# Attention's values, loaded once and placed a second time by a copy

## The chip, the cores and the metric

The kernel runs on one core of one Trainium2 chip. The metric is device time in microseconds (us); three runs of the kernel before gave a median of 1081.24 us, with 1080.13 and 1085.15 as the lowest and the highest. A core has five engines with a queue each: PE (TensorE, the matmuls; its weight loads are listed as PEld), DVE (VectorE), ACT (ScalarE), POOL (GpSimd) and SP (SyncE, which here only issues transfers). Each works through its own instructions in the order in which the program wrote them, and semaphores make one engine wait for another. Transfers run on 16 DMA engines, whichever queue issues them.

## What is computed

Sparse attention, and then a mixture of experts over its output. Attention has 8 batches, 8 heads, 576 positions and a head size of 64. A query of the first four heads sees the 32 positions up to and including its own; one of the last four sees every fourth position, again 32 of them.

```python
mask_plain = (rel >= 0) & (rel < window)                                  # window = 32
mask_dil = (rel >= 0) & (rel < window * dilation) & (rel % dilation == 0) # dilation = 4
scores = np.where(masks[None], scale * q @ k.T, -1e9)
attn = exp(scores - max);  attn = attn / (sum(attn) + 1e-09)
x = (attn @ v)                       # rows of 8 heads * 64 = 512, 4608 of them
# each row then goes to two of 8 experts: relu(x @ w1[e]) @ w2[e], weighted and added
```

After a regrouping of the positions, a dilated head is four plain ones, each on every fourth position. In both cases a query needs at most the keys and values of its own block of 32 and of the block before.

## The kernel before

**Groups and stages.** The batches are taken two at a time (four pairs). A pair has two groups: the dilated heads (even groups, `ty` = 1) and then the plain heads (odd groups, `ty` = 0), so there are 8 groups, and each has three stages, 24 in all (stage `k`, group `g` = `k` // 3). A stage multiplies queries and keys (`qk`, L371, on top of masks that L360 puts into PSUM), takes the maximum and the difference on DVE (L376, L377) and the exponential on ACT (`expo`, L382); in the next round PE transposes the exponentials and ACT brings them back (`ptr`, L396 and L397), PE multiplies them with the values (`pv`, L414), and DVE divides by the sum (L421 to L426). A round later the result is moved, stored and transposed, and the gate's matmul is done (`move_x` L434, `store_x` L439 and L441, `x_transpose` L449, `gate_mm` L471).

**The values.** A matmul in `pv` works on 64 queries' worth of two blocks at once. It contracts over 128 partitions: 64 keys for the first 32 queries (`w` = 0) and 64 keys for the second 32 (`w` = 1). The values stand in a tile of two halves along the partition, one for each `w`, and where a partition belongs to the other `w` there is zero, so that one matmul gives both results side by side. Before the change, even partitions belong to `w` = 0 and odd ones to `w` = 1. With blocks of 32 numbered along the sequence, `w` = 0 needs blocks 2n - 1 and 2n, and `w` = 1 needs 2n and 2n + 1: every block is used twice. The host lays the values out as such windows, with every block in it twice (`windows`), and a load fills every second partition. There is one tile for dilated groups (`VD`, shown as `vd`, 4680 fp32 on a partition for each `w`) and two for plain groups (`VP`, shown as `vp`, 2340 each). Zeros are written once: into `vd` by ACT (L139), into `vp` by DVE and POOL (L197).

**What sets the order.** The program is unrolled, and the order in which it calls the engines is the order of their queues. Work that isn't part of a stage hangs on numbered slots, two for each round (`at(slot, f)`, carried out by `fillers`). Group `g` begins at slot `s0` = 6 `g`; the loads of the next group's values hang on `s0` + 3, + 5 and + 7, those of the keys and queries two groups ahead on `s0` + 7 and later. All these loads are issued by SP, in one queue with the stores of the results, which wait for the stages. At slots 2, 4 and 5 stand `setup_a`, `setup_b` and `setup_c`, which prepare constants and the token table on POOL and DVE: `setup_b` begins with POOL's L232 to L242 (`tokc`, `tc`), and DVE's L237 and the lines after it read them. Three pieces of the table's padding follow at slots 6, 12 and 18 (`pads`, L281 to L284).

From about slot 17 on, the rows that are finished get their experts (`gate`), and POOL scatters an entry of a table for each (`fill_slots`, L628), at most four scatters a round; before the first of them POOL copies one element of the latest result (`pace`, L306), and so waits for it. Later POOL gathers the rows of the experts (L770, L778). The experts' matmuls (`up` L826, `down_tile` L868) begin when attention is over, at 227.2 us, and take the rest of the time.

Of the kernel before, what the change touches and what calls it, by code (L numbers as in the profile page):

```python
# [9 lines left out]
F32 = mybir.dt.float32  # L10
# [15 lines left out]
U = 4  # L26
# [14 lines left out]
US_W2 = 3.0, 3.5  # L41
LAG = 15
US_X = (17, 52)


@with_exitstack
def attention_moe_kernel(ctx, tc, qt, kp, kd, vpl, vdl, w_gate, w_noise, noise, w1, w2, out, CAPS=(1216, 1216, 1216, 1184, 1184, 1152, 1152, 1152), SPLITS=(0, 384, 896)):
    nc = tc.nc
    tensor, vector, scalar, gpsimd, sync = nc.tensor, nc.vector, nc.scalar, nc.gpsimd, nc.sync
# [32 lines left out]
    sm = actx.enter_context(tc.tile_pool(name="sm", bufs=2))  # L82
# [13 lines left out]
    VP = [vp.tile([128, 2, 9, 4, 65], F32, name=f"vp{i}") for i in range(2)]  # L96
    VD = dp.tile([128, 2, 9, 4, 2, 65], F32, name="vd")
# [5 lines left out]
    def qk_loads(g, parts=1):  # L103
        u, ty = g // 2, 1 - g % 2
        for i in range(parts):
            n = KN[ty] // parts
            for y in range(2):
                yield lambda i=i, n=n, y=y: sync.dma_start(
                    KT[ty][y:128:2, y, n * i:n * i + n], (kp, kd)[ty][u, y:128:2, n * i:n * i + n])
            n = 4 * S // parts  # L110
            yield lambda i=i, n=n: sync.dma_start(QT[ty][:, n * i:n * i + n], qt[u, ty, :, n * i:n * i + n])

    def v_loads(g):
        u, ty = g // 2, 1 - g % 2
        if ty:
            d = VD.rearrange("p w j h y c -> p w (j h y c)")
            n = d.shape[2] // 3
            for i in range(3):
                for w in range(2):
                    yield lambda i=i, w=w: sync.dma_start(d[w:128:2, w, n * i:n * i + n],  # L120
                                                          vdl[u, w:128:2, n * i:n * i + n])
        else:
            for b in range(2):
                for w in range(2):
                    yield lambda b=b, w=w: sync.dma_start(VP[b][w:128:2, w].rearrange("p j h c -> p (j h c)"),
                                                          vpl[u, b, w:128:2])

    scalar.preload_act_table_set("natural_log_exp_and_others")  # L130
    none = acon.tile([128, 1], F32, name="none")
# [2 lines left out]
    gpsimd.memset(KT[1][:, 1], 0.0)  # L134
    for f in qk_loads(0, 2):
        f()

    def clear_by_copy(t):
        scalar.copy(t, none.to_broadcast(list(t.shape)) if len(t.shape) == 2 else  # L139
                    none.unsqueeze(2).unsqueeze(3).to_broadcast(list(t.shape)))  # L140

    VF = VD.rearrange("p w j h y c -> p w (j h y c)")
    for w in range(2):
        clear_by_copy(VF[:, w])
    clear_by_copy(KT[0][:, 0])


# [45 lines left out]
            p0 = 64 * x + 32 * h  # L193
            gpsimd.tensor_copy(m[p0:p0 + 32, 6 * h], m0[p0:p0 + 32, 1])
    vector.memset(KT[0][:, 1], 0.0)
    for b, w, eng in ((0, 0, vector), (0, 1, gpsimd), (1, 0, gpsimd), (1, 1, gpsimd)):
        eng.memset(VP[b][:, w], 0.0)  # L197
    tri = consts.tile([128, 128], BF, name="tri")
    ones = consts.tile([128, 128], BF, name="ones")
    wg = acon.tile([128, 4, 32], F32, name="wg")  # L200
# [151 lines left out]
    SB, PE_, PT, XG, XT, GS = {}, {}, {}, {}, {}, {}  # L352
# [25 lines left out]
        SB[k] = a  # L378

    def expo(k):  # L380
        p = sm.tile([128, 6, 64, 2], F32, name="pe")
        scalar.activation(p.rearrange("p j c w -> p j w c"), SB.pop(k).rearrange("p y (j w) c -> p (y j) w c", w=2),  # L382
                          AF.Exp, scale=0.125)
        PE_[k] = p

# [510 lines left out]
    def plan(t, f, lag=None):  # L896

        if lag is not None:
            plan(t, lambda: plan(now[0] + lag, f()))
        else:  # L900
            heappush(due, (t, next(turn), f))
# [9 lines left out]
    def at(kb, *fs):  # L911
        fill.setdefault(kb, []).extend(fs)
# [3 lines left out]
    for g in range(2 * U):  # L916
        s0 = 6 * g
        if g + 1 < 2 * U:
            for i, f in enumerate(v_loads(g + 1)):
                at(s0 + 3 + 2 * (i // 2), f)  # L920
        if g + 2 < 2 * U:
            for i, f in enumerate(qk_loads(g + 2, 2)):
                at(s0 + 7 + 2 * (i // 3), f)
    fronts = {6 * u + 6 + st: (u, st) for u in range(U) for st in range(3)}
    def idx_late(before, a, b, then):
        while any(g in gens for g in before):
            yield 1
        for _ in range(IX_WAIT):
            yield 1
        idx_dma(0, a, b)  # L930
        then()
# [20 lines left out]
    def split_first(bi, t):  # L952
        xsplit(0, bi, t)()
        done[bi] += 1

    def x_block(bi):
        gens.insert(0, first_blocks(bi))
        if bi == 0:
            later(max(L0 + SL_W1 + 3 - slot[0], 0), lambda: new_x(0, 0))
            return  # L960
        for i, t in enumerate(range(BLS[0][bi][0], BLS[0][bi][1])):
            plan(US_X[bi - 1] + 3.0 * i, lambda t=t: split_first(bi, t))

# [3 lines left out]
    at(29, lambda: (new_idx(0), gens.append(idx_late(list(gens), 0, SPLITS[1], lambda: x_block(0)))))  # L967
    at(41, lambda: gens.append(idx_late(list(gens), SPLITS[1], SPLITS[2], lambda: x_block(1))))
    at(2, setup_a)
    at(4, setup_b)  # L970
    at(5, setup_c)
    for f in v_loads(0):
        f()
    for f in qk_loads(1):
        f()

# [18 lines left out]
    for kc in range(4):  # L995
        a, b = ((-3, 2), (-2, 3), (4, 6), (5, 7))[kc]
# [11 lines left out]
    for i in range(NS + 2):  # L1008
# [18 lines left out]
        if i < NS:  # L1027

            expo(i)
# [48 lines left out]
    for e in range(E):  # L1078
# [7 lines left out]
        t, at_ = start, {}  # L1086
# [4 lines left out]
        t = start if first else at_[0, 1]  # L1091
# [37 lines left out]
        if not last:  # L1129
            t = start + (42 if first else 20)  # L1130
            plan(t, lambda e=e: (new_idx(e + 1), idx_dma(e + 1, 0, CAPS[e + 1])))
            t = max(t + (14 if first else 9), at_[0, 1])
# [3 lines left out]
            t = at_[0, 2] + dur(e, 2, False)  # L1136
# [20 lines left out]
    with tc.If(big > 0):  # L1157
        with tc.For_i(0, E, 1) as r:
            e = nc.values_load(ci[0:1, bass.ds(r, 1)], min_val=0, max_val=E - 1)
            n = nc.values_load(ci[0:1, bass.ds(r + E, 1)], min_val=0, max_val=T - min(CAPS))  # L1160
# [22 lines left out]
def _layouts(q, k, v):  # L1183
    import numpy as np

    def heads(a, ty):

        a = a.reshape(U, 2, H, S, D)
        if ty == 0:
            return a[:, :, 0:4].reshape(U, 2, 2, 2, S, D).transpose(0, 5, 2, 1, 3, 4).reshape(U, 128, 2, 2, S)  # L1190
        a = a[:, :, 4:8].reshape(U, 2, 4, S // 4, 2, 2, D)
        return a.transpose(0, 6, 5, 1, 2, 4, 3).reshape(U, 128, 2, 4, S // 2)

    def windows(a):

        n = a.shape[1] // 64
        a = np.pad(a, ((0, 0), (32, 0)) + ((0, 0),) * (a.ndim - 2))
        p = np.arange(128)[:, None]
        at = 64 * np.arange(n) + p // 2 + 32 * (p % 2)
        return a[:, at]  # L1200

    qt = np.stack([heads(q, ty).reshape(U, 128, 4 * S) for ty in range(2)], 1)
    pad = ((0, 0),) * 4 + ((32, 0),)
    kp = np.pad(heads(k, 0), pad).reshape(U, 128, -1)
    kd = np.pad(heads(k, 1), pad).reshape(U, 128, -1)
    def with_ones(a):
        return np.concatenate([a, np.ones(a.shape[:-1] + (1,), np.float32)], -1)

    vpl = windows(with_ones(v[:, 0:4].transpose(0, 2, 1, 3))).reshape(U, 2, 128, -1)

    dil = v[:, 4:8].reshape(U, 2, 4, S // 4, 2, 2, D).transpose(0, 1, 4, 3, 2, 5, 6).reshape(U, S, 4, 2, D)
    vdl = windows(with_ones(dil)).reshape(U, 128, -1)
    return {"qt": qt, "kp": kp, "kd": kd, "vpl": vpl, "vdl": vdl}


# [18 lines left out]
```

## Time and profile before

| | us |
|---|---|
| median of three runs | 1081.24 |
| lowest and highest | 1080.13 and 1085.15 |
| span of the profiled execution | 1086.8 |
| attention: first mask matmul (L360) to the experts' first matmul | 9.6 to 227.2 |
| experts | 227.2 to the end |

The profiled execution is one run, recorded instruction by instruction. Its own time beside the span is not listed apart; its span is 5.6 us over the median of the runs. Of the span PE is busy for 1011.7 us (93%), DVE for 465.7, ACT for 319.4 and POOL for 534.5. The granted clock is the share of TensorE's full clock that it was given; its mean is 0.963.

A row of the timeline has the start, the time taken, the engine, the line, the operation, what it writes and reads, and the count; in brackets stands how long the engine was idle before it, and what ended that. A row of waits has the engine and line that waited, what for, the total, the count and the longest. "issue" means a wait for nothing that the profile shows, and "remote" a semaphore whose sender it doesn't show.

### The profile page before, as it was taken

To read this page: it belongs to the slowest core of one execution; us is meant where nothing else is said; L and a number is where in the kernel's file an instruction comes from. 1 tells how busy PE (TensorE), PEld (TensorE's weight loads), DVE (VectorE), ACT (ScalarE), POOL (GpSimd) and SP (SyncE) were. 2 spreads that over 40 slices of the span, in tenths; PEclk is the share of its full clock that TensorE was granted. 3 is DMA by queue.
4 is the path that set the end of the run, shared out by engine and by line. 5 is a ranking of instruction groups with operands and counts; after the bars stand their busy time and mean duration, and the time that the engine had idled before them with its cause. 6 is when DMAs were issued, how large, how long until landed. Compare 5 with 4: busy or idle time off the path is not lost. (4 is left out here: it accounts for less than half of the span.)

```text
span 1086.8 us, 18768 instructions
## 1 busy us (share of the span) xinstructions
PE 1011.7 (93%) x7274; PEld 855.7 (79%) x7275; DVE 465.7 (43%) x1060; ACT 319.4 (29%) x609; POOL 534.5 (49%) x727
## 2 busy tenths in 40 slices
PE   6896877778989999999999999999999999999996
PEld 4774655567878989988997889788978888888885
DVE  7673635635225444344434352435353434343221
ACT  6673534622113322222223131312131222222110
POOL 7004243455776655755644564466455645553112
PEclk9998887878999999999999999999999999999999
DMA  8898687455255243533533352426242623453123
GB/s 280 313 315 278 194 283 257 151 164 186 43 96 129 54 109 85 109 84 86 91 85 85 86 131 50 102 64 135 38 112 52 137 39 108 75 119 72 24 28 45
DMA packets 79214, 132.95 MB, mean 122 GB/s; under 512 B 31648, under 2 KB 41296, under 8 KB 77840
## 3 DMA queue, kind: packets, MB, share of 16 engines
q1 hardware_dynamic: 56768, 92.56, 27.6%
q0 software_dynamic: 22352, 39.15, 19.6%
q8 instruction: 58, 0.95, 0.4%
q14 instruction: 36, 0.29, 0.1%
HBM read 92.11 MB, written 39.54 MB: 121 GB/s over the span
## 5 line engine op out<-in xcount | busy, mean ns | idle before, releaser
L826 PE MATMUL up<-x,w1h 128*128 128x512 f32 (+4 forms) x1536 | 396.7, 344 | 10.9 <-issue 8.2
L778 POOL DMA_INDIRECT g<-xs,ixi x258 | 269.7, 1045 | 84.0 <-issue 78.6
L826 PEld LDWEIGHTS up<-x,w1h 128*128 128x128 f32 x1536 | 273.1, 189 | 37.2 <-issue 8.7
L826 PE MATMUL up<-x,w1l 128*128 128x384 f32 (+4 forms) x768 | 263.4, 343 | 0.0
L868 PE MATMUL dn<-w2h,hh 128*128 128x512 f32 x576 | 225.5, 392 | 0.0
L868 PE MATMUL dn<-w2l,hh 128*128 128x512 f32 x576 | 224.7, 390 | 0.0
L868 PE MATMUL dn<-w2h,hl 128*128 128x512 f32 x576 | 224.6, 390 | 0.0
L832 DVE SCALAR_TENSOR_TENSOR hl<-up,hh 128x384 fp32r<-128x384 f32 (+2 forms) x192 | 106.7, 557 | 249.1 <-ACT hh L830 187.0
L830 ACT ACTIVATE hh<-up 128x384 fp32r<-128x384 f32 (+4 forms) x192 | 94.6, 498 | 298.7 <-PE up L826 248.7
L845 POOL DMA_INDIRECT out_rows<-y,ixs x67 | 107.3, 1602 | 141.4 <-DVE y L877 119.0
L826 PEld LDWEIGHTS up<-x,w1l 128*128 128x128 f32 x768 | 145.4, 189 | 11.8
L877 DVE TENSOR_SCALAR y<-dn,ixs 128x512 f32<-128x512 f32 x63 | 47.3, 751 | 188.2 <-PE dn L868 163.5
L868 PEld LDWEIGHTS dn<-w2h,hl 128*128 128x128 f32 x576 | 108.4, 188 | 22.7
L868 PEld LDWEIGHTS dn<-w2h,hh 128*128 128x128 f32 x576 | 108.5, 188 | 22.0
L868 PEld LDWEIGHTS dn<-w2l,hh 128*128 128x128 f32 x576 | 108.5, 188 | 21.8
L797 ACT CAST x<-xr 128x512 fp32r<-128x512 f32 x67 | 40.5, 605 | 216.0 <-DVE xr L795 175.8
L306 POOL COPY spacer<-hh 1x1 f32<-1x1 f32 x72 | 26.4, 366 | 131.9 <-ACT hh L830 131.6
L628 POOL DMA_INDIRECT tab<-en,si x72 | 71.8, 998 | 36.1 <-issue 16.2
L798 DVE TENSOR_TENSOR x<-xr,x 128x512 fp32r<-128x512 f32 x67 | 44.7, 667 | 17.9 <-ACT x L797 12.4
L371 PE MATMUL s<-kt,qt 128*32 128x128 f32 x1152 | 41.2, 288 | 9.9 <-DMA qt<-in_qt 5.4
L371 PEld LDWEIGHTS s<-kt,qt 128*32 128x32 f32 x1152 | 32.5, 115 | 20.3 <-issue 19.6
L708 DVE TENSOR_TENSOR w1l<-ws,w1h 128x1024 fp32r<-128x1024 f32 x32 | 38.8, 1218 | 20.8 <-ACT w1h L706 10.9
(186 smaller groups left out, 867.2 us busy)
## 6 DMA issues: line engine op xcount, KB each, us to landing
ws<-in_moe_w SPq DMA_DIRECT2D x36, 512.0 KB
ws<-in_moe_w SPq DMA_DIRECT2D x112, 128.0 KB
out_rows<-zero SPq DMA_DIRECT2D x38, 256.0 KB
vd<-in_vdl SPq DMA_DIRECT2D x24, 390.0 KB
vp<-in_vpl SPq DMA_DIRECT2D x16, 585.0 KB
qt<-in_qt SPq DMA_DIRECT2D x14, 576.0 KB
xs<-x SPq DMA_DIRECT2D x24, 256.0 KB
kt<-in_kd SPq DMA_DIRECT2D x16, 320.0 KB
```

The lines of the kernel that those rows point to most:

```text
L371: tensor.matmul(s[32 * qd:32 * qd + 32, e], lhsT=QV[ty][:, b, x, 32 * ub:32 * ub + 32], rhs=KV[ty][:, :, b, x, 32 * ub:32 * ub + 64], star ...
L628: ins = gpsimd.indirect_dma_start(out=tab, out_offset=bass.IndirectOffsetOnAxis(ap=si[:, kq, t:t + 1], axis=0), in_=en[:, kq, t], in_offse ...
L708: return lambda: vector.tensor_tensor(b, s, a.bitcast(F32), op=OP.subtract)
L778: gpsimd.indirect_dma_start(out=g[:, j], out_offset=None, in_=xq, in_offset=bass.IndirectOffsetOnAxis(ap=IX[e][1][:, r0 // 32 + j:r0 // 32 ...
L797: scalar.copy(xh[:, :, o:o + rn], xr[:, :, 0:rn])
L798: return lambda: vector.tensor_tensor(xl[:, :, o:o + rn], xr[:, :, 0:rn], xh[:, :, o:o + rn].bitcast(F32), op=OP.subtract)
L826: tensor.matmul(p[:, 0:n], lhsT=a[:, 128 * f:128 * f + 128], rhs=b[:, kc, 0:n], start=(i == 0), stop=(i == 11))
L830: scalar.activation(hh[:, f, 0:n], p[:, 0:n], AF.Relu)
L832: vector.scalar_tensor_tensor(hl[:, f, 0:m], p[:, 0:m], 0.0, hh[:, f, 0:m].bitcast(F32), op0=OP.max, op1=OP.subtract)
L845: ins = gpsimd.indirect_dma_start(out=out, out_offset=bass.IndirectOffsetOnAxis(ap=sc[0:rn, t, 1:2], axis=0), in_=y[0:rn], in_offset=None, ...
L868: tensor.matmul(p[0:rn], lhsT=a[:, f, o:o + rn], rhs=b[:, f % 2], start=(i == 0), stop=(i == 23))
L877: vector.tensor_scalar(y[0:rn], p[0:rn], wsc, None, op0=OP.mult)
```

## The change

**Layout.** The contraction's partitions are ordered anew: partitions 0 to 63 belong to `w` = 0 and 64 to 127 to `w` = 1, and each quadrant of 32 partitions holds one block: 2n - 1 and 2n for `w` = 0, then 2n and 2n + 1 for `w` = 1. `expo` writes the exponentials in that order. The host lays out every block once (`blocks`), 64 rows instead of 128.

**Loads.** `v_load` fills the second quadrant (partitions 32 to 63, `w` = 0) and the fourth (96 to 127, `w` = 1), with a transfer of 32 partitions for each. A dilated group has three parts, a plain group two, and the parts stand at the same slots as before.

**The second place.** `v_repeat` fills the third quadrant with a GpSimd copy of the second (`w` = 1). The first quadrant takes the fourth's blocks, one step along: in groups 0 to 3 (`VCOPY` = 4) by another GpSimd copy, in groups 4 to 7 by a load from DRAM, issued with the other loads. The copies hang on the slot three after the load's. Those of group 0 stand ahead of the first round, behind the masks in POOL's queue.

**Zeros.** ACT clears, of `vd`, the halves that belong to the other `w` and the first block's place. For `vp`, `clear_plain` does the same on DVE and POOL; that of the second plain tile moves to slot 3. The loads of group 0 no longer stand behind ACT's clearing of the whole `vd`.

```diff
+    def v_load(g, i):
+        b, j0, j1 = v_parts(g)[i]
+        n = VB[1 - g % 2]
+        for w in range(2):
+            sync.dma_start(VF[1 - g % 2][b][32 + 64 * w:64 + 64 * w, w, n * j0:n * j1],
+                           v_source(g, b)[32 * w:32 * w + 32, n * j0:n * j1])
+
+    def v_repeat(g, i, w):
+        b, j0, j1 = v_parts(g)[i]
+        n, t = VB[1 - g % 2], VF[1 - g % 2][b]
+        if w:
+            gpsimd.tensor_copy(t[64:96, 1, n * j0:n * j1], t[32:64, 0, n * j0:n * j1])
+            return
+        j0 = max(j0, 1)
+        dst, src = t[0:32, 0, n * j0:n * j1], (n * (j0 - 1), n * (j1 - 1))
+        if g < VCOPY:
+            gpsimd.tensor_copy(dst, t[96:128, 1, src[0]:src[1]])
         else:
+            sync.dma_start(dst, v_source(g, b)[32:64, src[0]:src[1]])
...
     for f in qk_loads(0, 2):
         f()
+    for i in range(3):
+        v_load(0, i)
...
-    VF = VD.rearrange("p w j h y c -> p w (j h y c)")
-    for w in range(2):
-        clear_by_copy(VF[:, w])
+    clear_by_copy(VF[1][0][0:64, 1])
+    clear_by_copy(VF[1][0][64:128, 0])
+    clear_by_copy(VF[1][0][0:32, 0, 0:VB[1]])
...
-    for b, w, eng in ((0, 0, vector), (0, 1, gpsimd), (1, 0, gpsimd), (1, 1, gpsimd)):
-        eng.memset(VP[b][:, w], 0.0)
+    for i in range(3):
+        v_repeat(0, i, 1)
+        v_repeat(0, i, 0)
+
+    def clear_plain(b):
+        for w, eng in ((1, (vector, gpsimd)[b]), (0, gpsimd)):
+            eng.memset(VF[0][b][64 - 64 * w:128 - 64 * w, w], 0.0)
+        gpsimd.memset(VF[0][b][0:32, 0, 0:VB[0]], 0.0)
+
+    clear_plain(0)
...
-        p = sm.tile([128, 6, 64, 2], F32, name="pe")
-        scalar.activation(p.rearrange("p j c w -> p j w c"), SB.pop(k).rearrange("p y (j w) c -> p (y j) w c", w=2),
+        p = sm.tile([128, 6, 2, 64], F32, name="pe")
+        scalar.activation(p, SB.pop(k).rearrange("p y (j w) c -> p (y j) w c", w=2),
                           AF.Exp, scale=0.125)
...
-            for i, f in enumerate(v_loads(g + 1)):
-                at(s0 + 3 + 2 * (i // 2), f)
+            for i in range(len(v_parts(g + 1))):
+                s1 = s0 + 3 + 2 * i
+                at(s1, lambda g=g, i=i: v_load(g + 1, i))
+                for w in (1, 0):
+                    at(s1 + (3 if w or g + 1 < VCOPY else 0), lambda g=g, i=i, w=w: v_repeat(g + 1, i, w))
...
     at(2, setup_a)
+    at(3, lambda: clear_plain(1))
     at(4, setup_b)
```

Here `VF` is the list of the same tiles with the last dimensions made one, `VB` the elements of one step (260 in a plain group, 520 in a dilated one), `v_parts` gives each part's tile and its steps (of 9), and `v_source` the rows in DRAM.

More of the change, by code (lines that the diff above doesn't have):

```diff
@@ L43 @@
 US_X = (17, 52)
+VCOPY = 4
 @with_exitstack
@@ L111, in qk_loads, with v_parts, v_source @@
             yield lambda i=i, n=n: sync.dma_start(QT[ty][:, n * i:n * i + n], qt[u, ty, :, n * i:n * i + n])
[L113 to L118, printed above, removed]
-                for w in range(2):
-                    yield lambda i=i, w=w: sync.dma_start(d[w:128:2, w, n * i:n * i + n],
-                                                          vdl[u, w:128:2, n * i:n * i + n])
-        else:
[L123 to L126, printed above, removed]
+    VF = [[t.rearrange("p w j h c -> p w (j h c)") for t in VP], [VD.rearrange("p w j h y c -> p w (j h y c)")]]
+    VB = 4 * 65, 8 * 65
+    def v_parts(g):
+        return [(b, 0, 9) for b in range(2)] if g % 2 else [(0, 3 * i, 3 * i + 3) for i in range(3)]
+    def v_source(g, b):
+        return vpl[g // 2, b] if g % 2 else vdl[g // 2]
+    def v_load(g, i):
[14 more added lines that the diff above has]
+            gpsimd.tensor_copy(dst, t[96:128, 1, src[0]:src[1]])
+        else:
+            sync.dma_start(dst, v_source(g, b)[32:64, src[0]:src[1]])
     scalar.preload_act_table_set("natural_log_exp_and_others")
@@ L136, in attention_moe_kernel @@
         f()
+    for i in range(3):
+        v_load(0, i)
     def clear_by_copy(t):
-        scalar.copy(t, none.to_broadcast(list(t.shape)) if len(t.shape) == 2 else
-                    none.unsqueeze(2).unsqueeze(3).to_broadcast(list(t.shape)))
-    VF = VD.rearrange("p w j h y c -> p w (j h y c)")
-    for w in range(2):
-        clear_by_copy(VF[:, w])
+        scalar.copy(t, none[0:t.shape[0]].to_broadcast(list(t.shape)))
+    clear_by_copy(VF[1][0][0:64, 1])
+    clear_by_copy(VF[1][0][64:128, 0])
+    clear_by_copy(VF[1][0][0:32, 0, 0:VB[1]])
     clear_by_copy(KT[0][:, 0])
@@ L969, in attention_moe_kernel @@
     at(2, setup_a)
+    at(3, lambda: clear_plain(1))
     at(4, setup_b)
     at(5, setup_c)
-    for f in v_loads(0):
-        f()
     for f in qk_loads(1):
@@ L1192, in heads, with blocks @@
         return a.transpose(0, 6, 5, 1, 2, 4, 3).reshape(U, 128, 2, 4, S // 2)
[L1194 to L1200, printed above, removed]
+    def blocks(a):
+        n, s = a.shape[0], a.shape[1]
+        a = a.reshape((n, s // 64, 2, 32) + a.shape[2:])
+        return np.moveaxis(a, 1, 3)
     qt = np.stack([heads(q, ty).reshape(U, 128, 4 * S) for ty in range(2)], 1)
@@ L1207, in with_ones @@
         return np.concatenate([a, np.ones(a.shape[:-1] + (1,), np.float32)], -1)
-    vpl = windows(with_ones(v[:, 0:4].transpose(0, 2, 1, 3))).reshape(U, 2, 128, -1)
+    vpl = blocks(with_ones(v[:, 0:4].transpose(0, 2, 1, 3))).reshape(U, 2, 64, -1)
     dil = v[:, 4:8].reshape(U, 2, 4, S // 4, 2, 2, D).transpose(0, 1, 4, 3, 2, 5, 6).reshape(U, S, 4, 2, D)
-    vdl = windows(with_ones(dil)).reshape(U, 128, -1)
+    vdl = blocks(with_ones(dil)).reshape(U, 64, -1)
     return {"qt": qt, "kp": kp, "kd": kd, "vpl": vpl, "vdl": vdl}
```

## Prediction

> **What bounds the kernel now.** I read the page's totals and slices first, then the busy time by stretches, then the timeline, the waits, and the DMA issues.
>
> ```profile
> span 1086.8 us, 18768 instructions
> PE   6896877778989999999999999999999999999996
> PEclk9998887878999999999999999999999999999999
> DMA  8898687455255243533533352426242623453123
> ...
> 54.00:81.00 27.00, 25.94 (x578) 21.21 (x567) 19.91 (x78) 19.08 (x51) 0.43 (x1) 1.00 0.94 315
> 81.00:189.00 108.00, 79.70 (x1333) 59.09 (x1335) 48.84 (x182) 44.46 (x113) 40.69 (x73) 0.82 0.79 256
> 400.00:1086.00 686.00, 674.66 (x3376) 583.45 (x3374) 262.97 (x417) 155.81 (x261) 347.70 (x424) 1.00 0.39 81
> ```
>
> The columns of the last three rows are the stretch, its length, the busy time of PE, PEld, DVE, ACT and POOL, the granted clock, the DMA share and GB/s. The reader is to see three regimes. From 400 us on PE is busy 674.66 of 686 us at clock 1.00: the change touches nothing there. From 54 to 81 PE is busy 25.94 of 27 us although the DMA engines are busy 94% of the time: a full DMA by itself does not hold PE up. From 81 to 189 PE is busy 79.70 of 108 us at clock 0.82. So only attention can move, and whatever attention's end moves by, the experts behind it move by.
>
> ```profile
> 36.52 0.50 PE L360 MATMUL s<-mask,identb 128*128 128x512 bf16 x2
> 83.44 0.50 PE L360 MATMUL s<-mask,identb 128*128 128x512 bf16 x2
> 197.62 0.48 PE L360 MATMUL s<-mask,identb 128*128 128x512 bf16 x2
> ...
> PEld s L371 <- issue: 19.6, 28, 4.4
> DVE mx L376 <- remote: 20.6, 3, 8.4
> ACT pt L397 <- remote: 21.0, 4, 8.3
> PE s L371 <- DMA qt<-in_qt: 5.4, 2, 4.1
> ```
>
> The first rows are the mask matmuls that open attention stages 4, 12 and 23 (of 0 to 23). Eight stages take 46.9 us, 5.87 each; the next eleven take 114.2 us, 10.38 each. The excess is 11 x (10.38 - 5.87) = 49.6 us. The wait rows (total, times, longest) say how it looks: engines that wait for nothing the profile shows, or for something "remote". Among the waits of the first 320 us there is no compute instruction that waits for a load of values; a load of queries held PE for 5.4 us. So the values' bytes cost time only where they are in the way of something else.
>
> **The change: bytes.** In the stretch with the excess these are the DMA's rows:
>
> ```profile
> DMA packets 12299, 27.65 MB, mean 256 GB/s; under 512 B 2944, under 2 KB 7552, under 8 KB 11772
> ...
> vd<-in_vdl SPq DMA_DIRECT2D x12, 390.0 KB
> vp<-in_vpl SPq DMA_DIRECT2D x8, 585.0 KB
> ```
>
> Values are 12 x 0.390 + 8 x 0.585 = 9.36 MB of 27.65, and they belong to groups 4 to 7 (each group has six loads of the first kind or four of the second). Before, a group fills four quadrants of 32 partitions. After, groups 0 to 3 load two of four, half the bytes; groups 4 to 7 load two and eight ninths of a third, 0.722. So the stretch loses 0.278 x 9.36 = 2.6 MB, 9.4% of its bytes. What is that worth? The bound from below is nothing, since 54 to 81 runs at full pace with a DMA share of 0.94. The bound from above is the whole excess, 49.6 us. I take the excess to shrink as the bytes do, 9.4%: **4.7 us** gained. It is nearer to the lower bound because the stretch that is fuller with DMA shows no excess at all. In groups 0 to 3 the saving is larger, but it lies under a PE that is busy 25.94 of 27 us, so I cost it at nothing; if that cover were gone it would show only at the wait for queries, treated below.
>
> **The change: GpSimd at the start.** These are the rows of the first stages, POOL's and then what hangs on them:
>
> ```profile
> 3.71 1.24 SPq L108 DMA_DIRECT2D kt<-in_kd  x2
> 7.39 5.96 SPq L120 DMA_DIRECT2D vd<-in_vdl  x6
> 7.86 1.20 POOL L190 CAST mask<-m 128x1152 bf16<-128x1152 f32 x1
> 9.12 1.05 POOL L194 CAST mask<-m 32x64 bf16<-32x64 f32 x4
> 10.23 6.02 POOL L197 MEMSET vp<- 128x2340 f32 x3
> 16.20 0.19 POOL L212 MEMSET wg<- 128x128 f32 x1
> 18.23 1.84 PE L414 MATMUL o<-vd,pt 128*32 128x130 f32 x48 [0.46 <-ACT pt L397]
> ...
> 22.56 0.27 POOL L233 IOTA tokc<- 128x36 int32 x1
> 23.08 0.96 DVE L377 TENSOR_TENSOR a<-s,mx 128x768 f32<-128x768 f32 x1
> 23.95 0.28 DVE L237 TENSOR_SCALAR tc<-tokc 128x36 int32<-128x36 int32 x1
> 28.58 0.23 DVE L421 TENSOR_SCALAR den<-o 128x6 f32<-128x6 f32 x2
> 29.10 1.02 DVE L426 TENSOR_TENSOR x<-o,den 128x384 f32<-128x384 f32 x2
> 29.95 2.31 PE L371 MATMUL s<-kt,qt 128*32 128x128 f32 x48 [4.05 <-DMA qt<-in_qt]
> 30.16 0.83 ACT L434 COPY x<-x 32x256 f32<-32x256 f32 x2 [3.67 <-DVE x L426]
> 33.36 0.96 DVE L377 TENSOR_TENSOR a<-s,mx 128x768 f32<-128x768 f32 x1
> 33.39 0.86 ACT L397 COPY pt<-pp 128x512 f32<-128x512 f32 x2 [2.40 <-PE pp L396]
> 34.47 1.57 PE L414 MATMUL o<-vd,pt 128*32 128x130 f32 x44
> ```
>
> The point is the pair L233 and L237. DVE is free at 24.04 and runs the token arithmetic of setup_b, whose input POOL finished at 22.83: POOL has only 1.2 us in hand. The change puts work ahead of L233 on POOL. First, six copies, which wait for loads. Ahead of the first part of the values lie the keys and queries of group 0, 4 x 0.320 + 2 x 0.576 = 2.43 MB; with the part's own 0.39 MB that is 2.8 MB. From the first issue at 3.71 and at the stretch's rate below (0.28 MB per us) it lands at 13.7, and I add 1 us for the notice of its landing: 14.7. Bounds are 11.4, where PE received the first queries, and 18.2, where the values were used without a wait. The copies have 5 x 1560 + 1040 = 8840 elements a partition. A GpSimd copy of fp32 to fp32 of that size is not in the trace; L190 gives 1.04 ns an element (a cast), the memsets 0.86. I take the cast's, as it reads too: 9.2 us (bounds 7.6, and 13 if such a copy costs half as much again as the cast). That is 23.9. Then one memset of 2340 (2.0 us) and a short one of 260 (0.25) in place of the three: 26.2, where L212 stood at 16.20. Setup_a takes as long as it did (16.20 to 22.3, its three DMA issues among it): 32.3. Then comes the clearing of the second plain tile, moved behind it: 2 x 2.0 + 0.25 = 4.3, so 36.6. L232 and L233 end at 37.2. Setting 64 partitions costs what 128 do, as the length along a partition sets it; if it were less, 2 us would come off.
>
> So DVE stands from 24.04 to 37.2, and everything queued behind L237 with it: the rest of setup_b, the normalisation of stage 1 (L421, L426), and the softmax of stage 3. From there I go by the old durations. Setup_b 4.6 (23.95 to 28.58) gives 41.8; L421 to L426 1.5 gives 43.4. ACT moves x (0.83) and evacuates pt (0.86): 45.1, as those two waited for x before. Then o of stage 2 takes 1.9, the gate matmuls 0.5, and stage 4 opens at 47.5 instead of 36.52: **11.0 us** lost. Softmax of stage 3 (setup_c's 1.5, then 2 x 1.0) ends at 46.9, just inside that. The 4.05 us for which PE waited for queries are inside as well: with 1.17 MB less ahead of them the queries come earlier, but nobody can use them. The gate's weights, whose loads POOL now issues 10 us later, hold PE's queue to about 30.5, also inside. Over its bounds (landing, copy, memset) this term is 6 to 18.
>
> ```profile
> 0.00:27.00 27.00, 18.07 (x302) 11.83 (x303) 20.08 (x58) 18.63 (x21) 19.61 (x44) 1.00 0.80 280
> ...
> 12.50:16.00 3.50, 1.43 (x41) 0.85 (x34) 2.43 (x3) 0.95 (x1) 3.50 (x2) 1.00 1.03 425
> ```
>
> **The change: GpSimd later.** Groups 1 to 3 copy when POOL is idle (0.43 us of work between 54 and 81), so nothing. In groups 4 to 7 the copies are 6 x 1.6 + 4 x 2.4 = 19 us. POOL has 40.69 us of work in the 108 us of that stretch, so they fit. Behind a copy that waits for its load stand the scatters of the token table; they are waited for only much later, by the gathers. I take nothing, with 9 us as the upper bound: one copy of 2.4 us in the way in each of four groups. The new order of the exponentials' output and the contiguous partitions change no instruction's length that I can see: nothing. ACT's clears grow by one piece of 520 elements at 4.09 us per 4680, 0.5 us, before PE has any use for them.
>
> **Sum.** 1086.8 + 11.0 - 4.7 = 1093.1 in a profiled execution. The median of the runs is 1081.24, 5.6 less than this execution; the same offset gives **1087**.
>
> [...]
>
> **Rivals.**
>
> *The stalls go.* The excess is a matter of two things at once, scatters from POOL and a full DMA:
>
> ```profile
> 128.00:137.00 9.00, 8.38 (x198) 6.71 (x190) 7.98 (x51) 6.22 (x19) 2.22 (x4) 0.92 0.40 87
> 145.00:155.00 10.00, 5.09 (x44) 2.24 (x41) 0.21 (x2) 1.04 (x2) 6.54 (x13) 0.75 0.92 293
> ```
>
> POOL scatters in both stretches. Where the DMA share is 0.40, PE runs 198 matmuls in 9 us; where it is 0.92, 44 in 10 us. If lighter value loads leave half of such bursts with a free DMA, half the excess goes, 24.8 us, and with the start's 11.0 the time is 1081.2 - 13.8 = **1067**. It decides as soon as more than 11.0 of 49.6 us go. Against it: only 9.4% of the bytes go. Chance 0.28.
>
> *Loads into one quadrant are slow.* If they move at half of 425 GB/s, the values of 81 to 189 take 0.722 x 9.36 / 0.2125 = 31.8 us instead of 22.0, 9.8 us more on 85 us of DMA work (0.79 x 108), 11.5%; the excess grows by 5.7 instead of shrinking. With 11.0 and 0.9 us at the first part the time is 1081.2 + 17.6 = **1099**. Nothing above contradicts it. The nearest loads into 32 partitions in the trace are these; paced by their issue, they reach 202 GB/s in all, which fits both. Chance 0.13.
>
> ```profile
> DMA packets 192, 0.52 MB, mean 202 GB/s; under 512 B 64, under 2 KB 64, under 8 KB 192
> ...
> ws<-in_moe_w SPq DMA_DIRECT2D x3, 128.0 KB
> ```
>
> *The start's loss is absorbed.* If stages 12 to 23 go at a pace set by transfers and not by when they began, a late start meets shorter queues and the 11 us are won back: **1081**. For it: the DMA is full from 5 us on. Against it: no compute waits for value loads. Chance 0.12.
>
> **How the numbers follow.** The forecast has 0.42, with its own range 1081 to 1093 (the start's term at 6 to 13 and the excess by its share); the remaining 0.05 is for what I have not named. 0.5% is about what a measurement of this kernel can tell from no change, so slower begins at 1086.6 and faster ends at 1075.8. The forecast lies on that edge: 0.24 of its chance is slower, 0.18 the same. With the rivals, and 0.02, 0.02 and 0.01 of the remainder, slower has 0.24 + 0.13 + 0.02 = 0.39, the same 0.18 + 0.12 + 0.02 = 0.32, faster 0.28 + 0.01 = 0.29. The range reaches to the first rival's time and, above, short of the second's: 1067 to 1098.
>
> **What would show it.** Right: after six copies on POOL, the first token arithmetic (L237's line) starts near 37 with a wait for POOL of some 13 us before it, and stage 4 opens near 47.5. The bytes from group 4 on fall by about a tenth, and the later stages' mean is near 10 us. Wrong: DVE does not wait there, so the start's loss is not real; or the stages from 12 on take under 9.4 us each, where the saving outweighs the start; or packets of values last twice as long as before, where the second rival holds.

## The result and the profile after

The changed kernel takes 1124.56 us (median of four runs, 1123.72 to 1126.66), against 1080.68 us (1079.09 to 1085.15) for the kernel before on the same chip: ratio 1.0404, 95% interval 1.0373 to 1.0436. That is 43.9 us slower; 1087 us, with a range of 1067 to 1098, had been forecast. The profiled executions differ by 35.2 us (spans of 1122.0 and 1086.8).

The page of the kernel after has these totals and slices (each slice is 28.05 us):

```profile
span 1122.0 us, 18851 instructions
...
PE   7287778667899999999999999999999999999996
...
PEclk9598988977899999999999999999999999999998
DMA  8167948645525534444362425233533534363123
```

The second digit of PE is new: a stretch near 28 to 56 us in which PE hardly works, the DMA hardly moves (digit 1), and the granted clock falls (digit 5 in that slice, 0.60 over 27 to 54 us in the row below). From the thirteenth slice on PE's row stands at 9 up to the last slice, as in the page before. Because the diff adds 24 lines ahead of the loop, an old line number appears 24 higher below.

The busy time by stretches of the kernel after shows first that hole and then its stages 12 to 23 (columns as in the prediction):

```profile
27.00:54.00 27.00, 5.88 (x78) 4.52 (x78) 14.04 (x37) 1.81 (x7) 20.71 (x32) 0.60 0.19 45
118.10:234.70 116.60, 85.50 (x1428) 63.95 (x1425) 59.92 (x213) 48.63 (x123) 54.77 (x78) 0.88 0.72 208
```

and the same stages of the kernel before:

```profile
83.40:197.60 114.20, 85.24 (x1428) 63.27 (x1425) 54.19 (x209) 49.48 (x123) 40.69 (x73) 0.82 0.75 242
```

Stages 12 to 23 moved 208 x 116.6 = 24.3 MB instead of 242 x 114.2 = 27.6, 12% less, and took 2.4 us more, not 4.7 us less. PE's timeline after gives the openings of stages 4, 12 and 23, and the first matmul of the experts:

```profile
57.58 0.50 PE L384 MATMUL s<-mask,identb 128*128 128x512 bf16 x2
...
118.14 0.50 PE L384 MATMUL s<-mask,identb 128*128 128x512 bf16 x2
...
234.75 0.48 PE L384 MATMUL s<-mask,identb 128*128 128x512 bf16 x2
268.80 0.99 PE L850 MATMUL up<-x,w1h 128*128 128x384 f32 x2
```

Before, these stood at 36.52, 83.44, 197.62 and 227.24. So the lateness is 21.1 us at stage 4, 34.7 at stage 12, 37.1 at stage 23 and 41.6 at the experts. Five sixths of it is there by stage 12.

**Lost by stage 4.** POOL and DVE after, from their timelines:

```profile
16.79 1.48 POOL L136 COPY vd<-vd 32x1560 f32<-32x1560 f32 x1 [6.63 <-DMA vd<-in_vdl]
...
24.05 1.48 POOL L141 COPY vd<-vd 32x1560 f32<-32x1560 f32 x1
...
38.74 0.27 POOL L257 IOTA tokc<- 128x36 int32 x1
...
40.07 2.17 POOL L136 COPY vp<-vp 32x2340 f32<-32x2340 f32 x1
42.29 1.91 POOL L141 COPY vp<-vp 32x2080 f32<-32x2080 f32 x1
```

```profile
39.05 0.20 DVE L261 TENSOR_SCALAR tc<-tokc 128x36 int32<-128x36 int32 x1 [13.34 <-POOL tokc L257]
...
40.07 0.17 DVE L269 SCALAR_TENSOR_TENSOR tc<-tc,tc 128x9 int32<-128x9 int32 x1
40.17 2.09 DVE L268 TENSOR_SCALAR tc<-tokc 128x9 int32<-128x9 int32 x1
...
42.30 1.93 DVE L269 SCALAR_TENSOR_TENSOR tc<-tc,tc 128x9 int32<-128x9 int32 x1
```

DVE waited 13.34 us for POOL's iota: that is the wait the prediction named. Behind it stands something that it did not name. Operations of 9 elements that took 0.16 and 0.17 us in the kernel before took 2.09 and 1.93 us here beside a GpSimd copy, and ended as the copy ended (42.26 and 42.24; 44.23 and 44.20). With four of them held, setup_b took from 39.05 to 51.6, 12.5 us instead of 4.6.

**Lost between stages 4 and 12.** POOL, DVE and SP's queue after:

```profile
73.75 1.48 POOL L136 COPY vd<-vd 32x1560 f32<-32x1560 f32 x1 [24.98 <-DMA vd<-in_vdl]
75.28 1.05 POOL L141 COPY vd<-vd 32x1040 f32<-32x1040 f32 x1
76.28 0.41 POOL L305 MEMSET free<- 128x388 int32 x1
...
96.45 2.13 POOL L136 COPY vp<-vp 32x2340 f32<-32x2340 f32 x1 [9.48 <-PE o L438]
98.64 1.92 POOL L141 COPY vp<-vp 32x2080 f32<-32x2080 f32 x1
100.51 0.41 POOL L305 MEMSET free<- 128x392 int32 x1
```

```profile
76.73 0.27 DVE L306 COPY free<-free 128x194 int32<-128x194 int32 x1 [4.35 <-POOL free L305]
76.91 1.53 DVE L307 TENSOR_SCALAR free<-free 128x97 int32<-128x97 int32 x1
```

```profile
69.89 1.09 SPq L128 DMA_DIRECT2D vd<-in_vdl  x2
78.50 0.36 SPq L308 DMA_DIRECT2D tab<-free  x1
```

This is a chain over three queues. A copy waits on POOL: the first for its load; what ended the second wait is less clear, since PE's last matmul on `vp` had started at 73.2, and in the run with the padding moved the same wait ends with the load. The clearing of padding rows (L305) stands behind the copy on POOL; DVE's two operations on the padding wait for that, and the second of them takes 1.53 and 2.19 us beside the next copy instead of 0.26 (56.56). Behind these two, in DVE's queue, stands the division by the sum (L445 to L450), and PE waits for its result:

```profile
79.54 1.33 PE L473 MATMUL xtp<-ident,x 128*128 128x128 f32 x6 [2.45 <-DVE x L450]
...
106.18 1.51 PE L473 MATMUL xtp<-ident,x 128*128 128x128 f32 x6 [6.77 <-DVE x L450]
```

SP's store of the padding (L308) waits for DVE too, and later loads wait behind it in SP's queue, from 70.98 to 78.50 the first time; but in these two stages PE waits for no load, so that delay is not shown to cost anything here. Stage 7 took 10.9 us (74.34 to 85.22) and stage 10 took 15.3 (96.61 to 111.86); before they took 6.0 and 6.8. Those 13.3 us are nearly the whole of what was lost between stages 4 and 12 (34.7 - 21.1 = 13.6).

**Slower loads.** The DMA view gives the mean rate of a stretch in which nearly all that arrives is group 0's values, with the DMA engines busy throughout; first before (13.0 to 17.5 us), then after (13.2 to 17.7):

```profile
DMA packets 387, 1.91 MB, mean 424 GB/s; under 512 B 77, under 2 KB 77, under 8 KB 387
```

```profile
DMA packets 255, 1.10 MB, mean 245 GB/s; under 512 B 83, under 2 KB 83, under 8 KB 242
```

A packet of 6240 bytes of values took 238 ns before (median over the records of the first 60 us) and 404 ns after. So the loads ran at 0.58 of the rate, where the prediction's second rival assumed half, and the saving of bytes was mostly not a saving of DMA time.

### The profile page after: what moved, and what is told of

Read it like the earlier page. It is cut to its first block, busy times and chain, and to the rows that moved or that the text cites. A ratio compares the mean times of both kernels' runs of the same rounds, so it can differ in the third digit from the quotient of the medians.

```text
span 1122.0 us, 18851 instructions
## 1 busy us (share of the span) xinstructions
PE 1022.9 (91%) x7274; PEld 861.8 (77%) x7275; DVE 485.9 (43%) x1060; ACT 317.9 (28%) x610; POOL 582.5 (52%) x759
## 5 line engine op out<-in xcount | busy, mean ns | idle before, releaser
L802 POOL DMA_INDIRECT g<-xs,ixi x258 | 266.0, 1031 | 85.0 <-issue 80.2
L892 PEld LDWEIGHTS dn<-w2h,hh 128*128 128x128 f32 x576 | 108.1, 188 | 22.4 <-issue 0.5
L395 PE MATMUL s<-kt,qt 128*32 128x128 f32 x1152 | 46.3, 294 | 8.8 <-issue 8.4
L473 PE MATMUL xtp<-ident,x 128*128 128x128 f32 x144 | 23.7, 302 | 32.8 <-DVE x L450 25.6
L822 DVE TENSOR_TENSOR x<-xr,x 128x512 fp32r<-128x512 f32 x67 | 44.7, 667 | 17.9 <-ACT x L821 13.8
L395 PEld LDWEIGHTS s<-kt,qt 128*32 128x32 f32 x1152 | 34.9, 117 | 21.7 <-issue 21.0
```

What stands on the lines that cost most here:

```text
L395: tensor.matmul(s[32 * qd:32 * qd + 32, e], lhsT=QV[ty][:, b, x, 32 * ub:32 * ub + 32], rhs=KV[ty][:, :, b, x, 32 * ub:32 * ub + 64], star ...
L802: gpsimd.indirect_dma_start(out=g[:, j], out_offset=None, in_=xq, in_offset=bass.IndirectOffsetOnAxis(ap=IX[e][1][:, r0 // 32 + j:r0 // 32 ...
L822: return lambda: vector.tensor_tensor(xl[:, :, o:o + rn], xr[:, :, 0:rn], xh[:, :, o:o + rn].bitcast(F32), op=OP.subtract)
L892: tensor.matmul(p[0:rn], lhsT=a[:, f, o:o + rn], rhs=b[:, f % 2], start=(i == 0), stop=(i == 23))
```

## The experiments

Ratios compare with runs of the kernel before on the same chip, which took 1086 to 1091 us in these sets; the intervals are 95%. The change after has 1.0404 on this scale. Absolute times in the expectations belong to the first chip; they are read here by their ratios.

**GpSimd's part of the token arithmetic ahead of the copies.**

```diff
+    gpsimd.memset(tokc, 0)
+    gpsimd.iota(tokc[:, :, 3:4], ...)    # and the five iotas of v and s
     for i in range(3):
         v_repeat(0, i, 1)
         v_repeat(0, i, 0)
```

> GpSimd's part of the token arithmetic (the clearing of tokc and its six iotas) is issued ahead of the first six copies instead of behind them. Theory A (the loss sits at the start: DVE waits 13.3 us for POOL's iota, and then its small operations are each held for the length of a GpSimd copy, some 8 us more): DVE starts the token arithmetic near 26, ends it near 31, stage 4 opens between 38 and 42 instead of 57.6 (the gate's weights, still loaded late, may hold it), and the time falls from 1124.6 by 14 to 19 us, to 1106 to 1111. Rival B (the block layout itself is slow: loads into 32 partitions, values read from them): the time stays within 5 us of 1124.6.

Ratio 1.0294 (1.0262 to 1.0326). The wait went and 1.1 points of 4.04 with it, just short of what theory A said (1106 to 1111 of 1080.7 is 1.023 to 1.028), though the weak end of that lies inside the interval. Stage 4 opened at 45.7, not 38 to 42. The token arithmetic ran from 25.80 to 33.2; what came in its place is told by PE's wait, and by DVE's rows of setup_c beside group 1's copies:

```profile
PE pp L497 <- DMA wg<-in_moe_w_noise: 8.6, 1, 8.6
```

```profile
38.94 2.34 DVE L300 CUSTOM_DVE_ANT_0 free<-pc,free 128x584 uint16<-128x584 uint16 x1
41.32 1.92 DVE L301 TENSOR_SCALAR free<-free 128x292 int32<-128x292 int32 x1
```

The gate's weights, which POOL still loaded behind the copies, came next, and then the same holding of DVE (0.46 and 0.31 us in the kernel after). A queue's lateness had several customers; freeing one served the next.

**No copies at all.**

```diff
-                for w in (1, 0):
-                    at(s1 + (3 if w or g + 1 < VCOPY else 0), lambda ...: v_repeat(g + 1, i, w))
+    (likewise for group 0; the places are set to zero once)
```

> Leaves out a part of the computation: no second place is filled, neither by a copy nor by a load; those places hold zeros. GpSimd has no copies at all, and the values' bytes are half of those before in every group. Theory A: all of the loss goes, and what is left is the worth of the bytes: 1077 if the excess of stages 12 to 23 shrinks as the bytes do, near 1057 if half of the stalls go. Rival B (layout): over 1100 in spite of the missing work.

Ratio 1.0007 (0.9985 to 1.0029). The whole loss is gone, so the layout with half of the bytes does not cost it. But half of the values' bytes are gone as well, and they brought nothing, neither the 4 nor the 24 us that the two readings gave them. At the lower rate of the new loads (245 GB/s in the kernel after) this run alone doesn't say whether the bytes are worth nothing or the lower rate takes back what they bring; two later runs change one of the two at a time.

**Every second place by loads.**

```diff
-            gpsimd.tensor_copy(t[64:96, 1, ...], t[32:64, 0, ...])
+            sync.dma_start(t[64:96, 1, ...], v_source(g, b)[0:32, ...])
-VCOPY = 4
+VCOPY = 0
```

> The block layout with every second place filled by loads on SP's queue and no copy on GpSimd: as many bytes as before the change, in loads of 32 partitions. Theory A (the copies do the harm): 1081, within 5 us, and packets of values of 238 ns as before. Rival B, in the form of loads into one quadrant at half rate: packets near 480 ns and 1095 or more.

Ratio 1.0156 (1.012 to 1.0192), the rival's side. A packet of 6240 bytes had a median of 453 ns in the first 60 us (238 in the kernel before). Loads into single blocks of 32 partitions, carrying all the bytes, cost 1.6% by themselves. Most of it was lost early: stage 4 opened at 48.33, 11.8 us late, after PE had stood for 13.49 us ahead of stage 3's first matmul with queries (4.05 before).

**Group 1: memsets in place of copies.**

```diff
+        if g == 1:
+            gpsimd.memset(t[64:96, 1, ...] if w else t[0:32, 0, ...], 0.0)
+            return
```

> Leaves out a part of the computation: in group 1 alone GpSimd writes zeros into the second places (memsets of the same size) instead of copying them; all else as after the change. It tells whether a GpSimd instruction that reads SBUF is what holds DVE's small operations. If it is: the DVE operations of the token arithmetic beside them fall from 1.9 to 2.1 us each to 0.2, the token arithmetic takes near 5 us instead of 12.5, and stage 4 opens near 50 instead of 57.6. If any GpSimd instruction holds those of one kind (one SBUF input) and only a reading one those of the other (two SBUF inputs): four of 2.09 us stay, four of 1.93 go, stage 4 near 54. If DVE is slow there for another reason: stage 4 stays at 57.6.

Stage 4 opened at 55.4 (ratio 1.0363, 1.0329 to 1.0397). DVE's timeline decides, beside GpSimd memsets of 2.04 and 1.82 us:

```profile
38.98 1.96 DVE L276 TENSOR_SCALAR tc<-tokc 128x9 int32<-128x9 int32 x1
...
40.98 0.17 DVE L277 SCALAR_TENSOR_TENSOR tc<-tc,tc 128x9 int32<-128x9 int32 x1
41.08 1.74 DVE L276 TENSOR_SCALAR tc<-tokc 128x9 int32<-128x9 int32 x1
...
42.85 0.17 DVE L277 SCALAR_TENSOR_TENSOR tc<-tc,tc 128x9 int32<-128x9 int32 x1
```

The second case holds, though in the kernel after two operations of each kind had been held for 2.09 and 1.93 us, not four. The `scalar_tensor_tensor` with two SBUF inputs took 0.17 us beside a memset, after 1.93 beside a copy; the `tensor_scalar` with a single SBUF input took 1.96 and 1.74 us beside a memset and 2.09 beside a copy. Two further ones stood beside the later memsets (1.90 us for a pair that took 0.27 in the kernel before, and 1.47 instead of 0.18), so the arithmetic still took 11.2 us; of the 2.2 us by which stage 4 opened earlier, 1.3 are the arithmetic and the rest is an earlier start. Not every operation with one SBUF input was held: in the kernel after, L447's reciprocal took 0.23 us beside four copies. Nor were the operations that read PSUM: in the kernel after, ten of L445 ran beside copies at 0.15 us. With two SBUF inputs, then, the copies held the operation and the memsets did not; what sets the held operations with one SBUF input apart from the reciprocal is not shown.

**Half of the bytes, at the old rate.** The kernel before, without its loads for window 1:

```diff
-                    yield lambda i=i, w=w: sync.dma_start(d[w:128:2, w, ...], vdl[u, w:128:2, ...])
+                    yield lambda i=i, w=w: w or sync.dma_start(d[w:128:2, w, ...], vdl[u, w:128:2, ...])
```

> The kernel before the change, with the second half of its value loads (window 1) left out, so that a part of the computation is left out: those places hold zeros. Half of the values' bytes, in loads spread over all partitions as before, and nothing on GpSimd. It prices the bytes alone. The prediction's byte term (the excess of 49.6 us in stages 12 to 23 shrinks as the bytes do, here 4.68 of 27.65 MB, 17%): 8.4 us faster, ratio 0.992. Half of the stalls go: 25 us faster, ratio 0.977. Values' bytes are not what the excess is made of: ratio 1.000, within 0.003, and packets of 238 ns.

Ratio 0.9969 (0.9944 to 0.9995): 0.3%, between the third case and the first, nearer to the third. The DMA's mean rate from 12.6 to 15 us, when values arrive, was 424 GB/s, as in the kernel before. The stretch of its stages 12 to 23:

```profile
82.70:198.80 116.10, 86.44 (x1431) 64.01 (x1427) 54.34 (x209) 49.36 (x123) 40.85 (x73) 0.81 0.63 193
```

193 x 116.1 = 22.4 MB instead of 27.6, and 1.9 us longer in this execution. Here is no copy, no slow load and no late start. Half of the values' bytes can go and the 49.6 us of excess stay.

**The same loads into 64 neighbouring partitions.** The kernel before, with only the destination rows changed:

```diff
-    sync.dma_start(d[w:128:2, w, n * i:n * i + n], ...)
+    sync.dma_start(d[64 * w:64 * w + 64, w, n * i:n * i + n], ...)
```

> The kernel before the change, with the same value loads in number and bytes, but each into 64 neighbouring partitions (0 to 63 or 64 to 127) instead of every second of 128; the values land in the wrong rows, so the result is not the reference's, and all else is as before. Theory C (a load into neighbouring partitions of one half moves slower, whatever its rows): packets of 6240 bytes take near 400 ns instead of 238, and the kernel is 1.0 to 1.6% slower, as with every place filled by loads. Rival (it is only the loads of 32 rows, or the number of loads, that are slow): packets of 238 ns and ratio 1.000.

Ratio 1.0137 (1.0094 to 1.018): theory C. Its DMA view over 13 to 22 us:

```profile
DMA packets 394, 1.96 MB, mean 218 GB/s; under 512 B 76, under 2 KB 76, under 8 KB 394
```

The same loads in number, size and bytes reached 218 GB/s instead of 424, 0.51 of it, and a packet of 6240 bytes took 446 ns instead of 238. More than half of the price is paid at the start, where group 1's queries stand behind the slower values in SP's queue; PE's row for stage 3, which had a wait of 4.05 us before:

```profile
39.70 2.79 PE L371 MATMUL s<-kt,qt 128*32 128x128 f32 x48 [9.17 <-DMA qt<-in_qt]
```

Stage 4 opened at 46.67, 10.2 us late, while stages 12 to 23 took only 2.4 us more than before.

**The padding cleared by DVE.**

```diff
-            gpsimd.memset(padt, 0)
+            vector.memset(padt, 0)
```

> After the change, with one line moved: the clearing of the padding rows runs on DVE instead of GpSimd, so it no longer stands behind copies that wait for loads, and SP's queue no longer stands behind it. Theory D (this chain costs the two late openings of stages 8 and 11): stage 7 to 8 takes 6 us instead of 10.9 and stage 10 to 11 takes 7 instead of 15.3, and the time falls by about 12 us, ratio near 1.029 instead of 1.040. Rival (the loads are late for their own slowness, not for the queue): ratio stays within 0.003 of 1.040.

Ratio 1.0285 (1.0217 to 1.0354), 1.2 points less, as theory D had it. Stage 7 took 6.0 us (75.32 to 81.33); stage 10 still took 10.9 (92.72 to 103.66), not 7. So one of the two late openings went fully and the other by half. In what is left of stage 10, PE waited 2.41 us for DVE's `ob`, behind an operation in two parts that took 0.38 us in the kernel after and 2.13 here, beside a copy of 1.92 us:

```profile
100.86 2.13 DVE L588 TENSOR_TENSOR oh<-i,xf 128x72 f32<-128x72 f32 x2
```

**All of GpSimd's setup first, and the padding on DVE.**

```diff
+    setup_a()                      # was at(2, setup_a)
+    (the memset and iotas of setup_b, the two iotas of setup_c)
     for i in range(3):
         v_repeat(0, i, 1)
         v_repeat(0, i, 0)
     clear_plain(0)
```

> After the change, with all of GpSimd's own setup (the loads of the gate's weights, constants, the iotas of the token table and the padding) ahead of the first six copies, and the padding cleared by DVE. What is left of the change's cost are copies that hold DVE and the slower loads. Theory A with D: stage 3 opens at 26 to 28, stage 4 between 36 and 41, DVE waits nowhere over 2 us for GpSimd's iotas, and the ratio falls from 1.040 to 1.005 to 1.015. If the copies and the slow loads carry most of the loss: above 1.025.

Ratio 1.0222 (1.019 to 1.0253), between the two cases and near the second; its interval meets that of the run before. Stage 3 opened at 29.1, close to the bound, and DVE waited for no iota. Stage 4 opened at 51.1, far from 36 to 41. DVE's timeline:

```profile
27.64 1.17 DVE L254 TENSOR_SCALAR tc<-tokc 128x36 int32<-128x36 int32 x1
...
29.10 2.04 DVE L259 TENSOR_SCALAR tc<-tokc 128x9 int32<-128x9 int32 x1
...
35.82 1.93 DVE L260 SCALAR_TENSOR_TENSOR tc<-tc,tc 128x9 int32<-128x9 int32 x1
...
40.03 1.95 DVE L264 CUSTOM_DVE_ANT_0 tc<-tc 128x72 uint16<-128x72 uint16 x1
...
44.06 0.29 DVE L276 COPY tokc<-tc 128x36 int32<-128x36 int32 x2
```

Now that nothing waits, the arithmetic itself takes 16.6 us instead of 4.6: it meets GpSimd's clears (26.72 to 33.5) and then group 1's copies (33.58 to 41.9). The chain of short dependent DVE operations advanced here by about one hold for each long GpSimd instruction: three clears and four copies, seven holds, of 1.2 us for the first and 1.9 to 2.2 for the others.

**The later copies elsewhere.** From here on all kernels have the edit above. First, the copies of groups 1 to 7 on ACT:

```diff
-            gpsimd.tensor_copy(t[64:96, 1, ...
+            (scalar.copy if g else gpsimd.tensor_copy)(t[64:96, 1, ...
```

> As e9 (GpSimd's setup first, the padding cleared by DVE), with the copies of groups 1 to 7 on ACT instead of GpSimd; group 0's stay on GpSimd. Theory A2 (while GpSimd copies, DVE's small SBUF-to-SBUF operations stand; that is what was left in e9, where the token arithmetic took 16.7 us instead of 4.6): from 33.7 on the token arithmetic runs free and ends near 38 instead of 44.4, stage 4 opens near 43 instead of 51.1, the gate's small operations from stage 9 on are back to 0.2 us, and the ratio is 1.004 to 1.012 instead of 1.022. Rival (ACT, busy 70% of the early stages, becomes the bound, or waits for loads): stages of 7 us instead of 5.9 where copies are, ratio 1.015 or more.

Ratio 1.0326 (1.0289 to 1.0364): the rival. Stage 4 opened at 45.9, but stages 5 to 11 took 8.3 us each (56.5 to 114.6) instead of 5.9, and PE waited for ACT (total, times, longest, up to 130 us):

```profile
PE pp L481 <- ACT xt L461: 10.4, 4, 3.1
```

Then all copies on DVE:

```diff
-            gpsimd.tensor_copy(t[64:96, 1, ...
+            vector.tensor_copy(t[64:96, 1, ...
```

> As e9, with all copies on DVE, those of group 0 too, so that GpSimd and DVE meet only at the memsets of the plain tiles. Theory A2: nothing is held but the first token operations, stage 4 opens near 43, ratio 1.003 to 1.012. Rival (DVE is in order, so a copy that waits for its slow load holds the softmax behind it): openings of single stages over 4 us late with DVE waiting for loads of values, ratio 1.015 or more.

Ratio 1.0244 (1.0202 to 1.0287): the rival again. The first six copies wait for their loads ahead of the softmax, and stage 1 opened at 28.0 instead of 15.0:

```profile
PE s L370 <- DVE a L387: 15.4, 1, 15.4
```

Then without the copies and loads that fill the second places of groups 1 to 7:

```diff
-                for w in (1, 0):
-                    at(s1 + (3 if w or g + 1 < VCOPY else 0), lambda ...: v_repeat(g + 1, i, w))
```

> As e9, without the copies and loads that fill the second places of groups 1 to 7: a part of the computation is left out, those places hold zeros or old values. Theory A2 with C: what is left against before is the start alone (the memsets that hold the token arithmetic), stage 4 near 43, and ratio 1.003 to 1.008. If the loss of e9 is not the copies': ratio above 1.015.

Ratio 1.0031 (1.0001 to 1.006), as expected; so filling the places of groups 1 to 7, by GpSimd and by the loads of groups 4 to 7, carried 1.9 points of what was left. PE's timeline of this kernel, for stages 4, 12, 13 and 23:

```profile
43.97 0.54 PE L369 MATMUL s<-mask,identb 128*128 128x512 bf16 x2
...
90.84 0.50 PE L369 MATMUL s<-mask,identb 128*128 128x512 bf16 x2
102.25 0.81 PE L369 MATMUL s<-mask,identb 128*128 128x512 bf16 x2 [0.49 <-issue]
...
198.43 0.49 PE L369 MATMUL s<-mask,identb 128*128 128x512 bf16 x2
```

Stage 4 is 7.5 us late and stage 12 still 7.4. Stage 13 is 1.3 late (100.97 before) and stage 23 only 0.8: within stage 12 most of the lateness was absorbed.

**GpSimd's copies alone.** The kernel before, with its own loads, and the change's copies added:

```diff
+    for i in range(3):
+        v_repeat(0, i, 1)
+        v_repeat(0, i, 0)
     tri = consts.tile([128, 128], BF, name="tri")
...
+                        at(s0 + 6 + 2 * i, lambda ...: v_repeat(g + 1, i, w))
```

> The kernel before the change, with its own value loads, spread and with all their bytes, and beside them GpSimd's copies of the change, in the same number and sizes and at the same places in its queue (the six first ones ahead of its setup); they overwrite values, so the result is not the reference's. One part of the change alone. If the copies and their place carry the whole loss (the slow loads of half the bytes having cost nothing, as without any copies): token arithmetic held again, stage 4 between 45 and 58, ratio 1.025 to 1.045. If the loss needs both, copies that wait for slow loads: stage 4 as before, under 45, and ratio under 1.015.

Ratio 1.0309 (1.0242 to 1.0375), with stage 4 at 51.1: the copies carry about three quarters of the change's 4.04 points (2.4 to 3.8 by the interval), with the value loads of the kernel before and without the clears that the change also moved. The padding's chain is there too:

```profile
DVE free L307 <- POOL free L306: 11.0, 2, 7.7
```

## Why the prediction was wrong, step by step

**The bytes (-4.7 us): wrong.** The step read the excess of stages 12 to 23 as a cost of bytes, shared out by them. Half of the values' bytes at the old rate brought 0.3% (0.1 to 0.6), and half at the new rate without any copy brought nothing. Its argument for a low value, that a fuller stretch shows no excess, was an argument for no value at all. What the excess is made of stays open; in the trace before it lies beside POOL's scatters, but no run here took those away.

**The start (11.0 us, bounds 6 to 18): mechanism right, one term missing.** The wait came out as forecast: 13.34 us against 13.2, with the first copy at 16.79 (14.7 forecast, inside its bounds) and six copies in 8.7 us (9.2 forecast). The failed line is "From there I go by the old durations. Setup_b 4.6". Setup_b took 12.5 us, since four of its operations took 2.09 or 1.93 us beside GpSimd's copies. So stage 4 opened at 57.58, not 47.5, and the term was 21.1 us, above its upper bound: of the 10.1 us missing, 7.9 are setup_b, and most of the rest is the copies' later start, 16.79 against 14.7, where the 1 us added for the notice of a landing was the author's guess and no run shows it as a term of its own. Clearing 64 partitions took what 128 had taken, as forecast: 2.04 us for 2340 elements on GpSimd in either kernel. (By the prediction's own factor the upper bound of the copies is 13.8 us, not 13, and that of the term near 19, not 18; the measured term lies above either.)

**The loads of the gate's weights: as said.** They held PE until 32.77 (30.5 forecast), inside the longer wait; the first run shows that they are what comes next once that wait is gone.

**GpSimd later (0, bound 9): wrong.** "Groups 1 to 3 copy when POOL is idle, so nothing" looked at POOL's busy time and not at who stands behind a copy that waits. The padding's clearing stood there, and behind it DVE's queue with the division that PE needs: 13.3 us at two stages by the trace, 1.2 points by the run with the padding moved. The prediction looked for such a queue only in groups 4 to 7. There PE waits for the copies themselves, three times between 143 and 231 us, all within stages 12 to 22 (total, times, longest):

```profile
PE o L438 <- POOL vd L136: 6.7, 2, 3.4
...
PE o L438 <- POOL vp L136: 3.5, 1, 3.5
```

That is 10.2 us of waiting, near the bound of 9; since stages 12 to 23 took only 2.4 us more than before, what it cost by itself isn't shown. From stage 23 to the experts the kernel after took 34.1 us instead of 29.6. Over all profiled executions this stretch took 33.1 to 41.2 us in the six kernels with GpSimd copies in groups 4 to 7, and 28.6 to 32.8 in the eight without; the path by which they lengthen it was not followed.

In the prediction's own terms, then, the lateness of 41.6 us at the experts is 21.1 at the start (11.0 forecast), 13.6 between stages 4 and 12 (0 forecast), 2.4 in stages 12 to 23 (-4.7 forecast) and 4.5 after them (0 forecast). Against this the experts ran 6.4 us shorter in the profiled execution (853.2 against 859.6). That part varies by itself: over the profiled executions of all runs it took from 852.4 to 863.4 us.

**The rivals.** *The stalls go*: refuted, since half of the bytes brought 0.3% and left the stages' excess as it was. *Slow loads into one quadrant* (0.13): the loads were slower, 245 against 424 GB/s, but the price was not the rival's. Its half of 425 GB/s was an assumption that no row of the trace before showed; the runs gave 0.58 with these loads and 0.51 with those into 64 neighbours. The slower loads cost 1.4 to 1.6% where all the bytes were carried, and nothing that shows with half of them; and with only the destination rows changed it was paid mostly ahead of stage 4 (10.2 us), where the rival counted 0.9, and little in stages 12 to 23 (2.4 us). *The start's loss is absorbed* (0.12): shown for 7.5 us, in the run without later copies; the 34.7 us of the change were not.

**The sum.** By the runs, moving the padding, moving the setup and leaving out the later filling take 1.2, 0.6 and 1.9 of the 4.04 points, and 0.3 is left; the 0.6 is not clear of noise, as the intervals of its two runs meet. These are steps in one order; another order would share them out differently, since each run shows that a wait removed lets the next one through. Of the versions that compute everything, the nearest to the kernel before is the one with every place filled by loads, 1.6% slower; and half the bytes at the old rate, with work left out, brought 0.3%, so little is to be won here by bytes.

## What to carry to other kernels

An operation moved to an idle engine had three prices here beside its duration: what stood behind it in that queue while it waited for its inputs (DVE's 13.34 us for an iota), what it held elsewhere while it ran (operations of 0.17 us that took 1.93), and what the next engine in the chain waited for it (PE's 10.2 us in stages 12 to 22). Busy shares showed none of them: GpSimd was busy for 0.43 of the 27 us from 54 to 81 before the change, and the padding's chain began there. Follow the queue order, and count the short DVE operations that work from SBUF to SBUF beside the moved one. Before a saving of bytes is priced, ask at which rate the remaining bytes move: the same 64 rows went at 424 GB/s into every second partition and at 218 into 64 neighbours.

## What was not expected of the hardware

- A DVE operation of 0.17 us stood for 1.93 to 2.09 us beside a GpSimd copy of 1.91 to 2.17; beside a memset of that length, the one with two SBUF inputs took 0.17 again and the one with a single SBUF input stood for 1.74 and 1.96. In the kernel after no operation with a PSUM input that ran beside a GpSimd copy was held.
- A load of 64 rows into every second partition ran at 424 GB/s, the same one into 64 neighbours at 218; loads of 32 neighbours that alternate between the two halves reached 245.
- A GpSimd copy of fp32 took 0.95 ns an element over 32 partitions (1560 in 1.48 us), and ACT needed as much (1.49); DVE needed 0.96 us.
